# A fused attention and gated-FFN block on one core: five instruction lists written in a new order

## The chip, the core and the metric

The kernel runs on one core of a Trainium2 chip. The core's engines work side by side: TensorE (PE, matrix multiply; its weight loads are shown as PEld), VectorE (DVE), ScalarE (ACT), GpSimd (POOL) and SyncE (SP, which here only issues DMA transfers). Each takes its own list of instructions strictly in order and waits on semaphores for the others. The metric is the time of one execution on the device in microseconds, as the median of several runs.

## The reference

x has 2048 rows of 512 values, in bf16. One layer norm feeds two branches, and their results are added to x:

```python
xn = _layernorm(x)
return x + _A_ref(xn, A_wqkv, A_wo) + _B_ref(xn, B_w_gate, B_w_up, B_w_down)

# branch A: attention, 32 heads of 16; each position sees itself and
# 7 earlier ones at distances 2, 4, ... 14
qkv    = xn @ wqkv
logits = einsum("bhsd,bhswd->bhsw", q, kg) * 16 ** -0.5     # masked before the start
attn   = softmax(logits)
A      = einsum("bhsw,bhswd->bhsd", attn, vg) @ wo

# branch B: gated FFN of width 1376
B      = (gelu(xn @ w_gate) * (xn @ w_up)) @ w_down
```

## The kernel before

**Blocks.** The 2048 rows are worked in four blocks of 512 (b = 0 to 3). x comes in as eight pieces p = 0 to 7 of 256 rows, two per block; pieces 0 and 1 in two halves each. A task name carries the block or the row tile: ld_x3 is the load of piece 3, norm6 the last step of the layer norm of the sixth 128-row tile, counted from 0.

**A block's work.** The layer norm of x goes over DVE (blocks 0 and 1: bnst, bnag, sub, rstd, norm) or ACT (blocks 2 and 3), with the root on ACT or POOL (sq). Its result is transposed into xnT: in block 0 by PE (tpx, L899) and copied out of PSUM by ACT (evx, L919) and DVE (evy); in the other blocks by a DMA transpose on SP (trx p_t, L882). PE then computes

- q and k of block 0 per 128 rows (mma, mmt; L959), everything else of q, k, v in groups of four matmuls of 512 columns (mm b_which_g; which is 0 for q, 1 for k, 2 for v; L1009),
- gate and up products (fg b_j, fu b_j, j = 0 to 9; L1221; a last narrow piece fg b_10, L1260, and its up part inside er),
- the logits' sums over the products that DVE made (er b_3, L1078 and L1085),
- the down and output projections per 128 rows (acca, accb, accd, accw, L1306).

ACT moves PSUM results to SBUF (evq, evk, evv at L1020 or L986; gelu L1231; uev L1238 and L1276; fe L1339) and does the softmax's exp and ln. DVE makes the attention's products and sums (pr L1040, pa L1053, pv L1188, pw L1197, pz L1203), the softmax's other steps (mask, d1, d2, d4, d6), the gated product h (L1245) and the last additions fin. SP issues all transfers: the loads, ss (L1168) and sl (L1180), which send the probabilities to a scratch tensor in DRAM and back in spread form, ldxr (x again, for the last addition) and sto (the result).

**Memory that is shared.** PSUM has eight banks, handed out to mm, fg, fu, er (three at once) and acc groups in turn; a group can start only when the bank that it gets was emptied by ACT or DVE. x pieces have four slots in SBUF (XIN), xnT has three blocks.

**The order.** The program is not written out by loops. `G.task` collects 712 tasks with what they read and write; the dictionary ORDER gives, by hand, one list of names for each engine; `G.schedule` walks the lists with the planner's durations and latencies to find the order in which slots come free, and so which slot each item gets; `G.assign_sync` derives the semaphore waits; `emit_engine` writes each engine's instructions in the order of its list. The planner's numbers reach the chip only through the choice of slots and the waits that follow from it. The loads issue from SP in list order, and a wait of one holds all behind it:

```python
for (s, v) in t.waits:
    e.wait_ge(s, v)
ins = t.emit(e)
ins.then_inc(t.sem, 16 if eng_name == "sp" else 1)
```

A gate-weight load is also made to wait for the key weights:

```python
t_w = G.task("sp", "ld_w%s0" % nm, 0, mk(), wr=[I_w], prio=R_WG + (nm == "u"), nbytes=1280 * 1024)
t_w.deps.add(t_ld["wk"])
```

ld_wt0, ld_wt1 and ld_wt2 are the last 96 columns of the gate weights and 32 and 64 of the up weights.

Of the kernel before, what the change touches and what calls it, by code (L numbers as in the profile page):

```python
# [9 lines left out]
    LAT_X=0.08,  # L10
    LAT_S=0.03,
    TOL=dict(pe=0.6, act=-0.3, dve=0.0, pool=0.0, sp=0.0),
    DMA_ISSUE=0.48,
    DMA_FIXED=2.0,
    DMA_BPUS=330e3,
    ACT_SWITCH=1.35,
    PE_SLACK=0.0,
    PE_MODE_SWITCH=0.115,
    PE_DRAIN=0.2,
    DRAIN=0.1,  # L20
    PE_COLD_F=2.0,
    HAM_TAU=4.0,
    HAM_ENTER=0.52,
    HAM_EXIT=0.30,
)


class PeClock:

    def __init__(self, prm):  # L30
        self.tau = prm["HAM_TAU"]
        self.enter = prm["HAM_ENTER"]
        self.exit = prm["HAM_EXIT"]
        self.f = prm["PE_COLD_F"]
        self.avg = 0.0
        self.t = 0.0
        self.warm = False

    def run(self, start, dur, util):
        import math  # L40
        if start > self.t:
            self.avg *= math.exp(-(start - self.t) / self.tau)
            if self.warm and self.avg < self.exit:
                self.warm = False
            self.t = start
        left = dur
        total = 0.0
        while left > 1e-9:
            step = min(left, 0.2)
            real = step * (1.0 if self.warm else self.f)  # L50
            a = math.exp(-real / self.tau)
            self.avg = self.avg * a + util * (1.0 - a)
            if not self.warm and self.avg > self.enter:
                self.warm = True
            elif self.warm and self.avg < self.exit:
                self.warm = False
            total += real
            left -= step
        self.t = start + total
        return total  # L60

# [74 lines left out]
class Graph:  # L136
# [70 lines left out]
    def schedule(self, orders, params=None):  # L207
        prm = dict(PARAMS)
        prm.update(params or {})
        LAT_X, LAT_S = prm["LAT_X"], prm["LAT_S"]  # L210
# [12 lines left out]
        efree = dict((e, 0.0) for e in ENGS)  # L223
        act_table = None
        pe_mode = None
        pe_clock = PeClock(prm)
        dma_free = 0.0

        def rdy(t, p, od):
            if p.eng == t.eng and (p.eng == "pe" or od):  # L230
                return p.end
            return p.done + (LAT_S if p.eng == t.eng else LAT_X)

# [33 lines left out]
        for _ in range(len(self.tasks)):  # L267
# [23 lines left out]
            elif t.eng == "pe":  # L291
                sw = 0.0
                if t.mode is not None:
                    if pe_mode not in (None, t.mode):
                        sw = prm["PE_MODE_SWITCH"]
                    pe_mode = t.mode
                t.end = est + sw + pe_clock.run(est, t.dur, t.util)
                t.done = t.end + prm["PE_DRAIN"]
            else:
                t.end = est + t.dur  # L300
                t.done = t.end + prm["DRAIN"]
                if t.eng == "act" and t.table is not None:
                    act_table = t.table
# [85 lines left out]
    def report(self):  # L389
# [17 lines left out]
        "warm14 mma0_0 tpx0_1 mmt0_0 mmt0_1 mmt1_0 tpx1_0 mmt1_1 mmt0_2 tpx1_1 mmt1_2 mmt0_3 mmt1_3 "  # L407
        "mm0_2_2_0 mm0_2_1_0 fg0_0 mm0_2_0_0 fg0_1 fg0_2 fg0_3 fu0_0 fu0_1 mm0_2_3_0 fg0_4 fu0_2 fu0_3 fu0_4 "
        "fg0_5 mm1_1_0_0 mm1_0_0_0 fu0_5 fg0_6 er0_3 mm1_0_1_0 mm1_1_1_0 fg0_7 mm1_1_3_0 mm1_0_2_0 mm1_2_3_0 "
        "fg1_0 mm1_0_3_0 mm1_1_2_0 fg1_1 fu1_0 fu1_1 fu0_6 fu0_7 fg1_2 fu1_2 mm1_2_2_0 mm1_2_1_0 fg1_3 fu1_3 "  # L410
        "fg0_8 fg1_4 fu0_8 mm1_2_0_0 fg1_5 fg0_9 fu1_4 fu0_9 fu1_5 fg1_6 fg0_10 fu1_6 mm2_0_0_0 mm2_1_0_0 "
        "mm2_1_1_0 mm2_0_2_0 er1_3 fg1_7 mm2_0_3_0 mm2_0_1_0 fg1_8 mm2_1_3_0 mm2_2_0_0 fg2_0 mm2_1_2_0 accd2 "
        "fu1_7 accd1 mm2_2_2_0 fu1_8 acca0 fg1_10 mm2_2_3_0 accb0 fg2_1 fg2_2 accd3 fg2_3 fu2_0 fg1_9 fu2_1 "
        "mm2_2_1_0 fu2_2 fu2_3 er2_3 mm3_1_0_0 mm3_1_3_0 fu1_9 mm3_0_0_0 mm3_1_2_0 mm3_0_2_0 mm3_2_1_0 "
        "mm3_0_1_0 mm3_1_1_0 fg3_0 mm3_0_3_0 fg2_4 mm3_2_0_0 mm3_2_2_0 mm3_2_3_0 fu3_0 fu2_4 fg2_5 fg2_10 "
        "accd7 fu2_5 fg3_1 fu3_1 fg3_2 accd5 acca4 er3_3 fg2_6 accb4 accd6 fu2_6 fg2_7 fg2_8 fg3_10 fu2_7 "
        "fu3_2 fu2_8 fg3_3 fg3_4 fu3_3 fg3_5 fg2_9 fu2_9 fu3_4 fg3_6 fu3_5 fg3_7 fu3_6 fu3_7 fg3_8 fg3_9 "
        "fu3_8 accd11 acca8 accd10 fu3_9 accd9 accb8 acca12 accd13 accd14_0 accd14_1 accw14_0 accw14_1 "
        "accw13 accd15_0 accb12 accw15_0 accw12 accd15_1 accw15_1 accd15_2 accw15_2",
    "act":  # L420
        "c_tbl sx1 sq0 negm1 sxx1 sq1 evx0_0 evx0_1 evq0_0 sq2 evq0_1 evk0_0 evx1_0 sq3 evk0_1 bnst8 evx1_1 "
        "bnst9 evq0_2 evk0_2 evq0_3 evk0_3 ve8 sq6 vp8 sq4 bnag8 evv0_2_0 evv0_1_0 halo1 bnag9 evv0_0_0 va8 "
        "gelu0_0 bnst10 gelu0_2 uev0_0 bnst11 ve10 evv0_3_0 gelu0_1 vp10 gelu0_3 uev0_3 uev0_1 bnag10 "
        "evk1_0_0 evq1_0_0 gelu0_5 bnag11 gelu0_4 uev0_5 uev0_4 uev0_2 vb8 evq1_1_0 evk1_1_0 gelu0_6 gelu0_7 "
        "exp0 sub8 va10 evq1_2_0 vb10 ln0 sub11 d5_0 evk1_3_0 evq1_3_0 evv1_3_0 uev1_0 evk1_2_0 sub9 uev1_1 "
        "uev0_6 uev0_7 gelu1_1 gelu1_0 evv1_1_0 sub10 norm9 uev0_10b gelu1_3 evv1_2_0 gelu0_8 norm10 norm8 "
        "uev1_2 gelu1_2 norm11 gelu1_5 uev1_3 gelu1_4 bnst12 gelu0_9 uev0_9 uev1_5 uev0_8 uev0_10a bnst13 "
        "uev1_6 uev0_10c evv1_0_0 evq2_0_0 gelu0_10 evk2_1_0 ve12 evk2_0_0 vp12 evq2_2_0 bnag12 gelu1_6 "
        "uev1_4 evq2_3_0 gelu1_7 bnag13 evq2_1_0 halo2 evk2_3_0 exp1 bnst14 va12 bnst15 vb12 ve14 evk2_2_0 "
        "vp14 uev1_10b bnag14 ln1 uev1_7 d5_1 sub13 halv1 fe2 bnag15 uev1_8 va14 vb14 sub15 sub12 fe1 "  # L430
        "uev1_10c evv2_2_0 sub14 norm12 norm13 fe0 evv2_3_0 evv2_0_0 gelu2_2 gelu2_1 norm14 fe3 norm15 halo3 "
        "uev1_10a gelu2_0 gelu1_10 uev2_1 evv2_1_0 uev2_0 uev2_3 uev2_2 gelu1_8 uev2_10b uev2_10c gelu2_3 "
        "gelu1_9 evq3_0_0 evk3_0_0 evq3_2_0 evk3_3_0 evk3_2_0 evq3_1_0 exp2 halv2 evk3_1_0 uev1_9 evv3_0_0 "
        "evv3_3_0 ln2 evv3_2_0 evq3_3_0 d5_2 evv3_1_0 uev3_0 halv3 gelu2_5 uev2_10a gelu2_4 uev2_5 uev2_4 "
        "uev3_1 fe5 gelu2_10 gelu3_1 fe7 fe4 uev3_10c gelu3_2 gelu3_0 exp3 uev3_10b uev2_6 uev2_7 fe6 ln3 "
        "uev3_2 d5_3 uev2_8 gelu2_6 uev3_3 gelu2_7 gelu2_9 uev2_9 gelu2_8 gelu3_4 gelu3_5 uev3_5 gelu3_3 "
        "gelu3_6 uev3_6 uev3_4 uev3_7 gelu3_7 fe11 gelu3_10 fe10 gelu3_9 uev3_10a uev3_9 gelu3_8 uev3_8 fe8 "
        "fe9 fe13 fe12",
    "dve":
        "c_wdz bnst0 bnag0 sub0 rstd0 norm0 mean1 sub1 evy0_0 rstd1 norm1 evy0_1 bnst2 bnag2 sub2 rstd2 "  # L440
        "norm2 bnst3 bnag3 sub3 rstd3 norm3 bnst6 bnst4 bnst5 bnst7 bnag6 bnag5 bnag4 bnag7 sub4 sub5 sub6 "
        "sub7 pr0_1 rstd6 rstd4 norm7 norm5 norm6 pr0_0 norm4 pr0_3 pr0_2 pa0_0 pa0_1 pr1_0 mask d1_0 h0_1 "
        "d2_0 pr1_1 h0_2 d4a_0 d4b_0 d4c_0 pa1_0 d6_0 pr1_3 pr1_2 h0_3 rstd8 pa1_1 h0_0 h1_0 rstd10 pv0_1 "
        "pv0_0 pv0_2 pw0_1 h1_1 pv0_3 pw0_2 h0_4 d1_1 pw0_3 d2_1 pz0 h0_10 pr2_0 d4a_1 pr2_1 d4b_1 d4c_1 "
        "pr2_2 d6_1 pr2_3 pa2_0 rstd12 pa2_1 h1_3 fin2 h1_2 pv1_0 rstd14 pv1_2 pv1_3 pv1_1 h1_10 pw1_1 d1_2 "
        "pw1_2 d2_2 pw1_3 pr3_0 d4a_2 pz1 d4b_2 h1_4 d4c_2 pr3_2 pr3_3 fin1 d6_2 pr3_1 h2_0 pa3_0 pa3_1 fin0 "
        "h2_1 pa3_2 pv2_1 d1_3 h2_10 d2_3 fin3 pv2_0 h2_2 d4a_3 pv2_2 d4b_3 h3_0 d4c_3 pw2_1 d6_3 pw2_2 fin7 "
        "pv2_3 h2_3 pw2_3 h2_4 fin6 pz2 pv3_1 pv3_2 fin4 pv3_0 pv3_3 h3_2 fin11 h3_3 fin5 pw3_1 h3_1 h3_10 "
        "h3_4 fin10 pw3_2 fin8 pw3_3 fin9 pz3 fin14_0 fin14_1 fin13 fin15_0 fin15_1 fin12 fin15_2",
    "pool":  # L450
        "c_ones c_onef c_id c_vnpad c_idb c_eps c_mhalf c_e8a c_e8b c_e8c c_e8d c_ktpad c_mask0 c_mask1 "
        "c_utz sq8 sq10 sq12 sq14",
    "sp":
        "ld_x0_0 ld_x0_1 ld_wq ld_x1_0 ld_wk ld_x1_1 ld_wv ld_x2 ld_x4 ld_x3 ld_wg0 ld_wu0 ld_wt0 ld_wt1 "
# [10 lines left out]
def d_mm(n, cnt=1):  # L465
    return cnt * max(64, n) * 0.4213e-3


def d_act(n):
    return 0.10 + 0.00085 * n  # L470
# [10 lines left out]
def bass_parallel_sum__sliding_local_dilated__glu_gated_geglu__prompt_kernel(nc, A_x, A_wqkv, A_wo, B_x, B_w_gate, B_w_up, B_w_down, out, dbg=None, cfg=None):  # L481
# [42 lines left out]
    with contextlib.ExitStack() as es:  # L524
# [60 lines left out]
        G = Graph()  # L585
# [136 lines left out]
        for p in range(NP):  # L722
# [20 lines left out]
            def tp0(t, b=b, base=base):  # L743
                return -200 + 10 * t if b == 0 else base
# [676 lines left out]
```

## Time and profile before

| what | value |
|---|---|
| time, median of 3 runs | 184.19 us (184.12 to 184.24) |
| span of the profiled execution, first to last instruction | 182.8 us |
| PE busy | 178.0 us, 97% |
| DVE busy | 168.8 us, 92% |
| ACT busy | 129.3 us, 71% |
| POOL busy | 11.1 us, 6% |
| granted TensorE clock, mean | 0.999 |
| read from HBM, written to it | 14.71 MB, 3.15 MB |

The span leaves out 1.4 us around the instructions that the time has. PE's busy time counts a pipelined matmul until its modelled end, so two groups of four overlap by 0.16 us: a group lasts 1.03 us and the next starts after 0.863. Where the text gives the start of a single task, it is its first instruction's in the trace, matched to the name by its place in the engine's list.

### The profile page before, as it was taken

The numbers are of one execution on the slowest core, as the hardware profiler recorded it, in microseconds if no ns is written. First come the engines' busy times: TensorE is split into PE (matmuls) and PEld (weight loads), VectorE is DVE, ScalarE is ACT, GpSimd is POOL, SyncE is SP. The second block draws the span as 40 slices with busy tenths as digits, with TensorE's granted clock in tenths as the row PEclk, the third lists the DMA queues.
The fourth block names the chain that finished last, engine by engine and source line by source line (L and its number), as shares of the span: only waits on it lengthen the run. The fifth ranks groups of instructions, "written<-read, shape, count | busy, mean of one in ns | idle before, by whom it ended". The sixth has DMA issues, their size and how long they took to land.

```text
span 182.8 us, 2777 instructions
## 1 busy us (share of the span) xinstructions
PE 178.0 (97%) x1060; PEld 89.8 (49%) x1060; DVE 168.8 (92%) x169; ACT 129.3 (71%) x266; POOL 11.1 (6%) x23
## 2 busy tenths in 40 slices
PE   8799999999999999999999999999999999999994
PEld 2685444554444544444444555444444444444673
DVE  3769999999999999999999989999999999999932
ACT  5589977899899899869997596934396764145011
POOL 6000000104000000504000000000000000000000
PEclk9999999999999999999999999999999999999999
DMA  4999559610364000002742000136310246222333
GB/s 111 359 376 377 132 113 299 211 50 21 97 190 98 0 0 0 4 14 74 201 115 61 0 0 0 37 81 158 129 59 0 46 138 221 57 84 74 91 106 107
DMA packets 26220, 19.60 MB, mean 107 GB/s; under 512 B 13824, under 2 KB 23008, under 8 KB 26208
## 3 DMA queue, kind: packets, MB, share of 16 engines
q1 hardware_dynamic: 26208, 19.44, 36.3%
q8 instruction: 8, 0.13, 0.3%
q14 instruction: 4, 0.03, 0.1%
HBM read 14.71 MB, written 3.15 MB: 98 GB/s over the span
## 4 chain that ended last, share of the span: by engine, by line
PE 89%; DMA 8%; SPq 1%; issue 0%; DVE 0%; DVEq 0%
PE PS L1221 38%; PE PS L1306 28%; PE PS L1009 18%; DMA Wg<-in_B_w_gate_dram 5%; DMA Wqkv<-in_A_wqkv_dram 3%; PE PS L1260 2%; PE PS L1085 2%; PE PS L1078 1%; SPq L731 1%; SPq L687 0%; DVE OB L1350 0%; DVEq L376 0%
## 5 line engine op out<-in xcount | busy, mean ns | idle before, releaser
L1306 PE MATMUL PS<-Wd,HT 128*128 128x512 bf16 (+2 forms) x209 | 40.8, 345 | 0.0
L1221 PE MATMUL PS<-xnT,Wg 128*128 128x512 bf16 x160 | 39.6, 379 | 0.3 <-DMA Wg<-in_B_w_gate_dram 0.3
L1221 PE MATMUL PS<-xnT,Wu 128*128 128x512 bf16 x160 | 38.8, 379 | 0.0
L1009 PE MATMUL PS<-xnT,Wqkv 128*128 128x512 bf16 x160 | 37.8, 379 | 0.0
L1040 DVE TENSOR_TENSOR UNI<-QT,KT 128x4096 f16<-128x4096 bf16 x16 | 36.4, 2287 | 0.1
L1188 DVE TENSOR_TENSOR UNI<-VN,PT 128x4096 f16<-128x4096 bf16 x16 | 36.0, 2286 | 0.0
L1306 PEld LDWEIGHTS PS<-Wd,HT 128*128 128x128 bf16 x209 | 19.7, 98 | 19.0
L1238 ACT ACTIVATE UU<-PS 128x512 bf16<-128x512 f32 x40 | 22.8, 604 | 7.9 <-PE PS L1221 6.2
L1197 DVE TENSOR_TENSOR UNI<-UNI 128x4096 f16<-128x4096 f16 x12 | 27.4, 2286 | 0.0
L1009 PEld LDWEIGHTS PS<-xnT,Wqkv 128*128 128x128 bf16 x160 | 17.9, 114 | 16.9 <-ACT UU L1238 0.4
L1231 ACT ACTIVATE GG<-PS 128x512 bf16<-128x512 f32 x40 | 23.4, 600 | 2.5 <-DVE HT L1245 1.7
L1221 PEld LDWEIGHTS PS<-xnT,Wg 128*128 128x128 bf16 x160 | 15.4, 98 | 19.6 <-DMA Wg<-in_B_w_gate_dram 0.7
L1221 PEld LDWEIGHTS PS<-xnT,Wu 128*128 128x128 bf16 x160 | 15.7, 98 | 18.8
L1339 ACT ACTIVATE OB<-PS 128x512 bf16<-128x512 f32 x14 | 8.2, 594 | 21.8 <-PE PS L1306 21.8
L1053 DVE TENSOR_TENSOR UNI<-UNI 128x4096 f16<-128x4096 f16 x9 | 20.4, 2282 | 0.0
L1306 PE MATMUL PS<-Wo,OT 128*128 128x512 bf16 (+2 forms) x76 | 16.5, 345 | 0.0
L1245 DVE TENSOR_TENSOR HT<-GG,UU 128x1024 bf16<-128x1024 bf16 x20 | 13.6, 686 | 0.0
L832 POOL TENSOR_TENSOR sq<-ve,mhalf 128x2 bf16<-128x2 f32 x4 | 8.2, 2058 | 73.3 <-ACT ve L828 73.3
L1020 ACT ACTIVATE VN<-PS 128x512 bf16<-128x512 f32 x16 | 9.3, 594 | 2.5 <-PE PS L1009 2.5
L1306 PEld LDWEIGHTS PS<-Wo,OT 128*128 128x128 bf16 x76 | 7.2, 98 | 6.5
L1020 ACT ACTIVATE QT<-PS 128x512 bf16<-128x512 f32 x12 | 7.2, 597 | 3.2 <-PE PS L1009 3.2
L959 PE MATMUL PS<-xnT,Wqkv 128*128 128x128 bf16 x128 | 8.2, 219 | 1.2 <-DMA Wqkv<-in_A_wqkv_dram 1.0
(85 smaller groups left out, 153.9 us busy)
## 6 DMA issues: line engine op xcount, KB each, us to landing
PT<-pt_scratch SPq DMA_DIRECT2D x16, 256.0 KB, 4.0
XR<-in_A_x_dram SPq DMA_DIRECT2D x16, 128.0 KB, 2.4
out_dram<-OB SPq DMA_DIRECT2D x14, 128.0 KB, 2.0
Wqkv<-in_A_wqkv_dram SPq DMA_DIRECT2D x3, 512.0 KB, 5.6
XIN<-in_A_x_dram SPq DMA_DIRECT2D x6, 256.0 KB, 6.0
Wg<-in_B_w_gate_dram SPq DMA_DIRECT2D x1, 1280.0 KB, 8.8
Wu<-in_B_w_up_dram SPq DMA_DIRECT2D x1, 1280.0 KB, 11.6
Wd<-in_B_w_down_dram SPq DMA_DIRECT2D x1, 1280.0 KB, 7.7
```

The source lines that it names most:

```text
L832: "pool", "sq%d" % t, 7.0, lambda e, t=t, n=n: e.tensor_tensor(out=sq[:, t:t + n], in0=ve[:, t:t + n], in1=mhalf[:, 0:n], op=ALU.pow),
L1009: ins = e.matmul(PS[:, 512 * it.slot:512 * it.slot + 512], lhsT=wcols(which, kt, g), rhs=xnT[:, itx.slot, kt, :], start=(kt == 0), stop=(k ...
L1020: return e.activation(out=o, in_=PS[:, 512 * it.slot:512 * it.slot + 512], func=ACTF.Identity, scale=(QSC, 1.0, 1.0)[which])
L1040: return lambda e: e.tensor_tensor(out=UNI[:, it.slot, :, :], in0=bass.AP(QT, (itq.slot * 4 + g) * 512, [[NQT * 4 * 512, 128], [0, 8], [1, ...
L1053: return lambda e: e.tensor_tensor(out=UNI[:, i0.slot, :, :], in0=UNI[:, i0.slot, :, :], in1=UNI[:, i1.slot, :, :], op=ALU.add)
L1188: return lambda e: e.tensor_tensor(out=bass.AP(UNI, ito.slot * 4096, [[NUNI * 4096, 128], [2048, 2], [512, 4], [1, 512]]), in0=bass.AP(VN, ...
L1197: return lambda e: e.tensor_tensor(out=UNI[:, i0.slot, :, :], in0=UNI[:, i0.slot, :, :], in1=UNI[:, i1.slot, :, :], op=ALU.add)
L1221: ins = e.matmul(PS[0:M, 512 * it.slot:512 * it.slot + 512], lhsT=Wx[:, kt, j * 128:j * 128 + M], rhs=xnT[:, itx.slot, kt, :], start=(kt = ...
L1231: return lambda e: e.activation(out=GG[:, ito.slot, q, :], in_=PS[:, 512 * it.slot:512 * it.slot + 512], func=ACTF.Gelu_apprx_tanh)
L1238: return lambda e: e.activation(out=UU[:, ito.slot, q, :], in_=PS[:, 512 * it.slot:512 * it.slot + 512], func=ACTF.Identity)
L1245: return lambda e: e.tensor_tensor(out=HT[:, ito.slot, j - 1:j + 1, :], in0=GG[:, ig.slot, :, :], in1=UU[:, iu.slot, :, :], op=ALU.mult)
L1306: ins = e.matmul(PS[:, 512 * it.slot:512 * it.slot + CW], lhsT=(OT[:, ito.slot, q, ti * 128:(ti + 1) * 128] if kind == "o" else HT[:, ith. ...
```

## The change

All five lists of ORDER hold the same names as before, and the bodies of all tasks are the same. Four lists are in a new order (POOL's is only wrapped differently), and the planner's numbers are changed: its durations of single tasks, its latencies, starting times and DMA rates, and the clock model of PE is taken out. One consequence is that items can get other slots.

In SP's list ld_x3 comes ahead of ld_x1_1 and ld_x2, ld_wv behind ld_x2, and ld_x4 behind ld_wv, directly ahead of ld_wg0 as ld_x3 was. ld_x5, which stood directly behind ld_wt1, now stands behind the first transpose trx3_0. The lists, cut to their heads and to what the text speaks of:

```diff
     "pe":
-        "warm14 mma0_0 tpx0_1 mmt0_0 mmt0_1 mmt1_0 tpx1_0 mmt1_1 mmt0_2 tpx1_1 mmt1_2 mmt0_3 mmt1_3 "
-        "mm0_2_2_0 mm0_2_1_0 fg0_0 mm0_2_0_0 fg0_1 fg0_2 fg0_3 fu0_0 fu0_1 mm0_2_3_0 fg0_4 fu0_2 fu0_3 fu0_4 "
-        "fg0_5 mm1_1_0_0 mm1_0_0_0 fu0_5 fg0_6 er0_3 mm1_0_1_0 mm1_1_1_0 fg0_7 mm1_1_3_0 mm1_0_2_0 mm1_2_3_0 "
...
-        "accd7 fu2_5 fg3_1 fu3_1 fg3_2 accd5 acca4 er3_3 fg2_6 accb4 accd6 fu2_6 fg2_7 fg2_8 fg3_10 fu2_7 "
-        "fu3_2 fu2_8 fg3_3 fg3_4 fu3_3 fg3_5 fg2_9 fu2_9 fu3_4 fg3_6 fu3_5 fg3_7 fu3_6 fu3_7 fg3_8 fg3_9 "
-        "fu3_8 accd11 acca8 accd10 fu3_9 accd9 accb8 acca12 accd13 accd14_0 accd14_1 accw14_0 accw14_1 "
-        "accw13 accd15_0 accb12 accw15_0 accw12 accd15_1 accw15_1 accd15_2 accw15_2",
+        "warm14 mma0_0 tpx0_1 mmt0_0 mmt0_1 mmt1_0 tpx1_0 mmt1_1 mmt0_2 tpx1_1 mmt1_2 mmt0_3 mm0_2_0_0 mmt1_3 "
+        "mm0_2_2_0 mm0_2_1_0 fg0_0 fg0_1 fg0_2 fg0_3 fu0_0 fu0_1 fu0_2 fg0_4 fu0_3 mm1_0_0_0 mm1_1_0_0 "
+        "mm0_2_3_0 fg0_5 fu0_4 fg0_6 mm1_1_1_0 er0_3 mm1_0_1_0 fg1_0 fg0_7 mm1_1_2_0 fu0_5 mm1_1_3_0 "
...
+        "mm3_1_1_0 fg2_7 fu3_1 accd7 fg3_2 fg3_3 fu3_2 mm3_2_2_0 acca4 er3_3 fg3_4 accb4 accd5 fu2_7 "
+        "mm3_2_1_0 fg3_5 fu3_3 fg2_8 fu2_8 fu3_4 accd6 fg3_6 fg3_10 fu3_5 fg2_9 fg3_7 fu3_6 fu2_9 fu3_7 fg3_8 "
+        "fu3_8 fg3_9 fu3_9 acca8 accb8 accd9 accd10 accd11 accd14_0 accd13 accd14_1 acca12 accw14_0 accw13 "
+        "accw14_1 accb12 accw12 accd15_0 accw15_0 accd15_1 accw15_1 accd15_2 accw15_2",
     "act":
-        "c_tbl sx1 sq0 negm1 sxx1 sq1 evx0_0 evx0_1 evq0_0 sq2 evq0_1 evk0_0 evx1_0 sq3 evk0_1 bnst8 evx1_1 "
-        "bnst9 evq0_2 evk0_2 evq0_3 evk0_3 ve8 sq6 vp8 sq4 bnag8 evv0_2_0 evv0_1_0 halo1 bnag9 evv0_0_0 va8 "
-        "gelu0_0 bnst10 gelu0_2 uev0_0 bnst11 ve10 evv0_3_0 gelu0_1 vp10 gelu0_3 uev0_3 uev0_1 bnag10 "
...
-        "gelu3_6 uev3_6 uev3_4 uev3_7 gelu3_7 fe11 gelu3_10 fe10 gelu3_9 uev3_10a uev3_9 gelu3_8 uev3_8 fe8 "
+        "c_tbl sx1 sq0 negm1 sxx1 sq1 evx0_0 evx0_1 evq0_0 sq2 evx1_0 sq3 evk0_0 evq0_1 evk0_1 evx1_1 evq0_2 "
+        "bnst8 evk0_2 sq4 evq0_3 sq6 bnst9 evk0_3 ve8 vp8 bnag8 halo1 bnag9 evv0_2_0 gelu0_0 gelu0_3 gelu0_2 "
+        "evv0_0_0 bnst10 uev0_0 uev0_1 bnst11 va8 uev0_2 gelu0_1 gelu0_4 ve10 evq1_0_0 vp10 uev0_3 bnag10 vb8 "
...
+        "d5_3 gelu3_5 gelu3_4 fe6 uev2_8 gelu2_8 uev3_4 uev3_5 gelu2_9 uev3_10b evv3_1_0 gelu3_6 uev2_9 "
+        "gelu3_7 uev3_7 uev3_6 gelu3_10 uev3_9 uev3_10c uev3_10a uev3_8 gelu3_9 fe8 gelu3_8 fe9 fe10 fe11 "
     "dve":
-        "norm2 bnst3 bnag3 sub3 rstd3 norm3 bnst6 bnst4 bnst5 bnst7 bnag6 bnag5 bnag4 bnag7 sub4 sub5 sub6 "
-        "sub7 pr0_1 rstd6 rstd4 norm7 norm5 norm6 pr0_0 norm4 pr0_3 pr0_2 pa0_0 pa0_1 pr1_0 mask d1_0 h0_1 "
...
-        "pv2_3 h2_3 pw2_3 h2_4 fin6 pz2 pv3_1 pv3_2 fin4 pv3_0 pv3_3 h3_2 fin11 h3_3 fin5 pw3_1 h3_1 h3_10 "
-        "h3_4 fin10 pw3_2 fin8 pw3_3 fin9 pz3 fin14_0 fin14_1 fin13 fin15_0 fin15_1 fin12 fin15_2",
+        "bnst3 bnag3 sub3 rstd3 norm3 bnst6 bnst4 bnst5 bnag6 bnag4 bnag5 bnst7 sub5 sub4 bnag7 sub6 sub7 "
+        "rstd4 rstd6 norm5 norm7 norm6 norm4 pr0_2 pr0_3 pr0_0 pr0_1 pa0_1 h0_0 pa0_0 pr1_0 mask rstd8 d1_0 "
...
+        "d6_3 pw2_1 h3_1 fin6 pw2_2 h3_2 pw2_3 h2_4 h3_0 h3_3 pz2 pv3_1 pv3_0 fin8 pv3_3 h3_4 h3_10 pv3_2 "
+        "pw3_1 fin10 pw3_2 fin11 pw3_3 fin9 pz3 fin14_0 fin14_1 fin13 fin15_0 fin12 fin15_1 fin15_2",
     "sp":
-        "ld_x0_0 ld_x0_1 ld_wq ld_x1_0 ld_wk ld_x1_1 ld_wv ld_x2 ld_x4 ld_x3 ld_wg0 ld_wu0 ld_wt0 ld_wt1 "
-        "ld_x5 trx3_1 trx2_1 trx3_0 trx2_0 ld_wt2 ld_x6 ld_wd0 ldxr2 ld_x7 ld_wd1 ldxr1 ld_wo ss0_0 ss0_1 "
-        "ss0_3 ss0_2 sl0_1 sl0_0 sl0_2 trx4_1 sl0_3 trx5_0 trx4_0 trx5_1 ss1_0 ss1_3 ss1_2 ss1_1 sl1_0 sl1_2 "
-        "sl1_3 trx6_1 trx6_0 sl1_1 trx7_0 trx7_1 ldxr0 sto2 sto1 ldxr6 ss2_0 ss2_1 ss2_3 ss2_2 sl2_1 sl2_0 "
...
+        "ld_x0_0 ld_x0_1 ld_wq ld_x1_0 ld_wk ld_x3 ld_x1_1 ld_x2 ld_wv ld_x4 ld_wg0 ld_wu0 ld_wt0 ld_wt1 "
+        "trx3_0 ld_x5 trx3_1 ld_wt2 trx2_0 trx2_1 ld_x6 ld_wd0 ss0_3 ss0_2 ss0_0 ss0_1 ld_wd1 sl0_1 sl0_2 "
+        "sl0_0 sl0_3 ld_wo ld_x7 trx4_1 trx4_0 trx5_0 trx5_1 ldxr0 ss1_3 ss1_2 ss1_0 ss1_1 sl1_1 ldxr2 sl1_0 "
+        "sl1_2 sl1_3 trx7_0 ldxr3 trx6_1 trx7_1 ldxr1 trx6_0 ldxr7 ss2_1 sto0 ss2_2 ss2_0 ss2_3 sl2_0 sto1 "
...
-SCHED = dict(DMA_BPUS=290e3, DMA_FIXED=1.7)
...
-        G.schedule(ORDER, SCHED)
+        G.schedule(ORDER)
```

## The prediction

> **What bounds the kernel now.** I read the page's busy line first, then the chain of waits, then the timelines of PE, ACT, DVE and SP over the first 30 us.
>
> From the page, each engine's busy time:
>
> ```profile
> PE 178.0 (97%) x1060; PEld 89.8 (49%) x1060; DVE 168.8 (92%) x169; ACT 129.3 (71%) x266; POOL 11.1 (6%) x23
> ```
>
> PE has 4.8 us without work in 182.8, DVE 14. From the chain that ended last (start us, length us, what):
>
> ```profile
> 2.75 5.60 DMA Wqkv<-in_A_wqkv_dram
> 8.35 0.02 issue
> 8.37 8.76 DMA Wg<-in_B_w_gate_dram
> 17.13 0.05 issue
> 17.17 1.04 PE PS L1221 x4
> 18.21 0.86 PE PS L1009 x4
> ...
> 24.25 4.32 PE PS L1221 x20
> 28.57 1.73 PE PS L1009 x8
> ...
> 163.53 16.75 PE PS L1306 x122
> ```
>
> The key weights land at 8.35 and release the gate weights, which land at 17.13. From 17.17 to 180.28 the chain is PE alone, with no wait between pieces. A reordering can't shorten this stretch: the same matmuls, at 0.863 us for a group of four, take the same 163 us. What can be won is PE work moved ahead of 17.17. What can be lost is any wait inside the stretch. The PE timeline just before it:
>
> ```profile
> 12.04 3.16 PE L959 MATMUL PS<-xnT,Wqkv 128*128 128x128 bf16 x48
> 15.03 1.89 PE L1009 MATMUL PS<-xnT,Wqkv 128*128 128x512 bf16 x8
> 17.17 1.04 PE L1221 MATMUL PS<-xnT,Wg 128*128 128x512 bf16 x4 [0.25 <-DMA Wg<-in_B_w_gate_dram]
> ```
>
> The two L1009 groups could have been followed by a third at 15.03 + 2 x 0.863 = 16.75; PE stood until 17.17, so 0.42 us. Smaller waits hide in the merged rows: the L959 batch mmt0_2 starts at 10.89, behind the first ACT row here, and mmt0_3 at 13.22, behind the last. ACT's timeline:
>
> ```profile
> 10.25 0.59 ACT L919 ACTIVATE xnT<-PS 128x512 bf16<-128x512 bf16 x1
> ...
> 11.96 0.63 ACT L769 ACTIVATE XS<-XIN 128x512 bf16<-128x512 bf16 x1 [0.45 <-DMA XIN<-in_A_x_dram]
> ...
> 12.59 0.58 ACT L919 ACTIVATE xnT<-PS 128x512 bf16<-128x512 bf16 x1
> ```
>
> evx1_0 (10.25) and evx1_1 (12.59) move transposed x out of PSUM. The second stands behind bnst8, which waited for x4. From DVE's timeline:
>
> ```profile
> 12.71 2.47 DVE L750 BATCH_NORM_STATS2 st<-XIN 128x6 f32<-128x512 bf16 x4 [1.10 <-DMA XIN<-in_A_x_dram]
> ```
>
> DVE waits 1.10 us for x3, which is in the queue behind x4. And from SP's timeline, the loads ld_wt1, ld_x5, the four block-1 transposes and ld_wt2:
>
> ```profile
> 9.99 2.62 SPq L703 DMA_DIRECT2D Wt<-in_B_w_up_dram  x1
> 12.66 4.04 SPq L737 DMA_DIRECT2D XIN<-in_A_x_dram  x1
> 19.26 5.23 SPq L882 DMA_TRANSPOSE xnT<-XIN  x4
> 24.53 0.58 SPq L703 DMA_DIRECT2D Wt<-in_B_w_up_dram  x1
> ```
>
> An issue of these kinds takes 0.43 to 0.6 us when nothing holds it. ld_wt1 ends at 12.61 as x3 lands (12.68), ld_x5 at 16.70 as Wg lands (17.13): SP is let in only when an older load is nearly down.
>
> **The change, part by part.** Durations are those of the profiled execution; its span of 182.8 stands 1.4 below the median of 184.19, and I add each difference in the span to the median.
>
> *Planner numbers, durations, byte counts.* No instruction comes or goes; they cost 0, and act only through the slots and waits that the planner derives.
>
> *Head, loads.* The weight and x bytes queued ahead of Wg are the same, and Wg still waits for wk (8.35), so I keep 17.13 for Wg and 20.41 for Wu. The rows' landings give 0.75 us per 256 KB (x2 11.18, x4 11.93, x3 12.68) and 0.35 for the 128 KB behind wk. In the new order: x3 9.10, x1_1 9.45 (was 8.70), x2 10.2, wv 11.9 (was 10.43), x4 12.7. x4 now takes the slot that waits for tpx0_1, as x3 did.
>
> *Head, ACT and DVE.* bnst3 starts at 9.5 instead of 9.25. sq3 no longer stands behind evk0_0, so norm3 ends near 11.35 (was 11.61), and bnst6 starts at 11.25 instead of 12.71. All four block-1 norms now stand ahead of the first pr0: from 11.25, 2.4 (four bnst) + 0.33 (bnag) + 1.05 (sub) + 0.2 + 1.05 (norm) give 16.3, and norm6, third of them, about 16.2 (was 19.75). evx1_0 starts at 10.0 and ends 10.57; evx1_1 follows three evictions from 10.65 and ends 12.66.
>
> *Head, PE.* mmt0_2 at 10.67 (-0.22); mmt0_3 at 12.71 (a batch costs 0.89, a transpose 0.23); then mm0_2_0_0, new ahead of Wg and with wv long landed, mmt1_3, and two L1009 groups: 12.71 + 0.92 + 0.86 + 0.89 + 0.86 + 0.86 = 17.10. Wg is there at 17.17, so fg0_0 starts as before, but mm0_2_0_0 (was at 18.05) is done. **Gain 0.86**; bounds 0.5, if PE gets there 0.35 late, and 0.9, which is the three waits together (0.22 + 0.29 + 0.42). fu0_0, four groups on, is at 20.62, 0.2 behind Wu.
>
> *Block 1 brought forward.* In the new PE list nine groups lie between 17.17 and mm1_0_0_0 (fg0_0 to fg0_3, fu0_0 to fu0_2, fg0_4, fu0_3): 17.17 + 9 x 0.863 = 24.94. Before, the first block-1 group was at 28.41, 2.7 us behind the last transpose's landing (25.73). Now all four transposes must be down by 24.9, and PE, in order, does nothing else meanwhile. On SP, trx3_0 takes the place directly behind ld_wt1 and stands ready at 16.2; then ld_x5, trx3_1, ld_wt2, trx2_0, trx2_1: each transpose 1.26, x5 0.45, wt2 0.6. *If nothing is held after 16.70*: trx3_0 ends 17.9, x5 18.4, trx3_1 19.65, wt2 20.25, trx2_0 21.5, trx2_1 22.8; a transpose lands 1.24 after its issue ends (24.49 to 25.73), so 24.05, and PE waits 0. *If x5 is held until Wu is down*, as the two held rows suggest (each went in with three weight pieces or so still unlanded; here Wu, two Wt pieces and a transpose are ahead): x5 ends about 20.0, trx3_1 21.25, wt2 21.85, trx2_0 23.15, trx2_1 24.45, landed 25.7; PE waits 0.8. I take the second, since two rows show it, and keep 0 and 1.2 (landing at 26.1, held until the Wt pieces land as well) as ends.
>
> [...]
>
> *ld_x5 later.* ACT's bnst10 stands behind gelu0_0, gelu0_3, gelu0_2 and evv0_0_0, at 22.4; x5 lands at 22.1 to 23.0 (issue end + 2.0 to 2.9, the latter as for x6, 25.67 to 28.53). ACT then runs back to back to about 58 in the new list. Counting banks at these spacings, PE still finds one of the 8 in time if x5 is down by 23.1, later by whatever PE has already waited. Cost 0; beyond, 1 us per us.
>
> *The later lists.* ACT keeps its table loads (sqrt, then gelu and exp in turn per block), er and acc groups are as many, DVE has 1.2 us in hand from the head. ldxr, ss and sl issues follow their data: ss0 starts with d6_0 at about 42 (was 43.46), so sl0_1 lands before 50.7, when pv0_1 wants it; trx5_1 lands near 60.5, mm2_1_0_0 is at 61.6; ldxr1 is put ahead of trx6_0, which still lands near 98, 4 us early. These cost 0, hidden by PE's own run. Two relays become tight: pa3_2 to er3_3 (0.66 before, about 0.25 now) and pz2 to acca8 (4.5 before). The latter: from fu3_7's start to acca8's PE has 5 x 0.863 = 4.32 us; ACT and DVE need until then 0.2 (fu2_9's end) + 0.48 x 3 (uev2_9, gelu3_7, uev3_7) + 0.60 (uev3_6) + 0.64 (h3_3) + 1.22 (pz2) + 0.1 (handoffs) = 4.2. I take 0 for both, with 0.4 as the upper end. The tail behind accw14_0 is the same chain of fin and store: 0.
>
> *Sum.* -0.86 + 0.8 + 0 = -0.06: 184.19 - 0.06 = 184.1. With the ends: -0.9 gives 183.3; -0.5 + 1.2 + 0.4 gives 185.3.
>
> **The rivals.**
>
> *B, the transposes land in time.* For it: trx3_1 in the old trace, issued at 19.26 with Wu unlanded, took 1.30 against 1.19 to 1.27 elsewhere, so hardly held. Against: by then Wu was nearly through. PE keeps the gain and, earlier everywhere, meets tighter banks and relays: -0.86 + 0.2 = 183.5.
>
> *C, the relay at acca8.* h3_3 is late by more than 0.15, since ACT or DVE has one more 0.5 us eviction or part of a 2.2 us product ahead, and PE waits for pz2 just ahead of accd9. It decides from 0.15 on, 1 us per us: at 0.7 late, with A's stall, 184.1 + 0.55 = 184.7. For it: DVE at 92% has no room to catch up, and the slack went from 4.5 us to 0.15. Against: my spacings are medians and the list may have room that I don't see.
>
> *D, x5 or the transposes later still*, landing past 26.5: 185.1.
>
> *That the change does not do what is said*: in SP's list x4 stays ahead of ld_wg0, and what moves is x5, from directly behind ld_wt1 to behind trx3_0. Both places are behind the gate weights. If that move counted for nothing, the head alone would remain, which is B.
>
> **How the numbers follow.** A, head gained and lost again at mm1_0_0_0: 0.42, within 183.7 to 184.6, time **184.1**. B 0.25, C 0.25, D 0.08. For eight in ten the range takes A, most of B and C up to 0.9 late: 183.4 to 185.0. About 0.2%, 0.37 us, is what a measurement here tells from no change. Faster, below 183.82: 0.21 of B and 0.08 of A, 0.29. Slower, above 184.56: 0.22 of C, 0.08 of D, 0.07 of A, 0.37. Within: 0.34.
>
> **What would show it.** PE: fg0_0 near 17.2 behind three L1009 groups instead of two, with no wait at mmt0_3 (else the head is wrong). A PE wait on a DMA of xnT near 25 of 0.3 to 1.2 (A); none (B). SP: the issue of x5 longer than 1.5 us, ending near 20 (A), or 0.45 long (B). ACT's wait for x5 below 0.7. Waits of PE L1306 or L1085 on DVE after 120 mean C. Wg landing away from 17.13 by more than 0.4 would upset the sum at its root.

## The result, and the profile after

The changed kernel is slower: 185.03 us median (184.87 to 185.25, 5 runs) against 184.24 for the kernel before beside it, ratio 1.0042, 95% interval 1.0029 to 1.0054. On a second occasion it was 184.78 (12 runs) against 184.04 (17 runs), 1.0036 (1.0021 to 1.0050). The forecast was 184.1, no change. One execution of all those below ran at a lower granted clock (0.991, 188.62 us) and is left out of the second experiment's figures. In the two profiles shown here PE was through earlier than before: its last group starts at 179.42 (before 179.88). That lead belongs to the profile before, whose gate weights landed late; in three later profiles of the old order the group starts at 178.86 to 179.41. PE's end does not show where the time went.

From the page after, each engine's busy time:

```profile
PE 177.2 (97%) x1043; PEld 89.8 (49%) x1060; DVE 169.0 (92%) x169; ACT 128.3 (70%) x266; POOL 18.4 (10%) x23
```

The work is the same; 17 matmul records are missing, so PE's figure is low by them, and PE's tasks below are placed by the weight loads, of which none is missing. POOL's 7 us more are its four sq tasks, one of them above all (last section). From the chain that ended last (start us, length us, what):

```profile
17.74 2.37 SPq L839
...
22.02 2.80 DMA xnT<-XIN
24.82 0.05 issue
24.87 2.78 PE PS L966 x12
...
126.07 2.21 DVE UNI L1010
128.28 0.04 issue
128.32 0.62 PE PS L1035 x16
```

Before, the chain ran over PE alone from 17.17 on. Now it enters PE at 24.87 from a transpose (mm1_0_0_0 waits for trx2_1) and at 128.32 from DVE (er3_3 waits for pa3_2). PE's timeline at the start of both stretches:

```profile
13.52 0.81 PE L966 MATMUL PS<-xnT,Wqkv 128*128 128x512 bf16 x3
14.16 1.06 PE L916 MATMUL PS<-xnT,Wqkv 128*128 128x128 bf16 x16
15.06 1.89 PE L966 MATMUL PS<-xnT,Wqkv 128*128 128x512 bf16 x8
16.78 3.62 PE L1178 MATMUL PS<-xnT,Wg 128*128 128x512 bf16 x16
...
128.32 0.62 PE L1035 MATMUL PS<-xnT,Wt 128*32 128x256 bf16 x16 [0.26 <-DVE UNI L1010]
```

Three groups (L966) now stand ahead of fg0_0, as forecast, and fg0_0 starts at 16.78, 0.24 behind the gate weights. SP's timeline, from the first transpose on (trx3_0, ld_x5, trx3_1, ld_wt2, trx2_0 and trx2_1 together with the gap between them):

```profile
15.76 1.30 SPq L839 DMA_TRANSPOSE xnT<-XIN  x1
17.11 0.57 SPq L694 DMA_DIRECT2D XIN<-in_A_x_dram  x1
17.74 2.37 SPq L839 DMA_TRANSPOSE xnT<-XIN  x1
20.15 0.58 SPq L660 DMA_DIRECT2D Wt<-in_B_w_up_dram  x1
20.78 2.90 SPq L839 DMA_TRANSPOSE xnT<-XIN  x2
```

SP's held issue ends at 20.11, 0.29 behind the landing of the up weights (19.82), but it is trx3_1, not ld_x5. Then the end. The DMA view of 180.2 to 183.2 us, first of the kernel before (queue, kind, packets, MB, share; then the issues: KB each and us from issue to landing):

```profile
q1 hardware_dynamic: 432, 0.20, 22.7%
...
out_dram<-OB SPq DMA_DIRECT2D x1, 32.0 KB, 1.6
```

and of the changed kernel:

```profile
q1 hardware_dynamic: 384, 0.15, 18.3%
q14 instruction: 1, 0.01, 0.6%
...
out_dram<-OB SPq DMA_DIRECT2D x1, 32.0 KB, 2.4
```

The last store, sto15_2, takes 2.4 us instead of 1.6, and there is a packet of another kind: 8 KB of *instructions*. By the packet records it starts at 181.31 and takes 0.31; behind it the last eight of the store's 128 data packets go out from 181.61 to 181.77, when all others had ended by 181.34. The store lands 2.08 us after its issue ended, 1.13 before. In the kernel before a packet of this kind comes at 184.54, 1.8 us behind the last instruction. A hint of where it comes from is in the lists: the new order makes DVE wait for more semaphores in instructions of their own, 193 instructions in DVE's trace instead of 188. ACT's has seven more too, 293 instead of 286.

### The profile page after: what moved, and what is told of

Read it like the earlier page. It is cut to its first block, busy times and chain, and to the rows that moved or that the text cites. A ratio compares the mean times of both kernels' runs of the same rounds, so it can differ in the third digit from the quotient of the medians.

```text
span 183.1 us, 2768 instructions
## 1 busy us (share of the span) xinstructions
PE 177.2 (97%) x1043; PEld 89.8 (49%) x1060; DVE 169.0 (92%) x169; ACT 128.3 (70%) x266; POOL 18.4 (10%) x23
## 4 chain that ended last, share of the span: by engine, by line
PE 34%; DVE 21%; ACT 20%; issue 11%; POOLq 4%; SPq 3%; DMA 3%; POOL 0%; DVEq 0%
PE PS L1263 18%; PE PS L1178 10%; DVE UNI L1010 5%; DVE UNI L1145 5%; POOLq L481 4%; DVE UNI L997 4%; ACT GG L1188 3%; DVE UNI L1154 3%; PE PS L966 3%; ACT UU L1195 3%; SPq L839 3%; PE PS L916 2%; DMA xnT<-XIN 2%; ACT XIN L810 1%; ACT XS L726 1%
## 5 line engine op out<-in xcount | busy, mean ns | idle before, releaser
L1178 PE MATMUL PS<-xnT,Wg 128*128 128x512 bf16 x158 | 38.9, 379 | 0.3 <-issue 0.2
L966 PE MATMUL PS<-xnT,Wqkv 128*128 128x512 bf16 x155 | 37.9, 379 | 0.5 <-issue 0.2
L966 PEld LDWEIGHTS PS<-xnT,Wqkv 128*128 128x128 bf16 x160 | 17.8, 114 | 17.2 <-DMA xnT<-XIN 0.6
L1195 ACT ACTIVATE UU<-PS 128x512 bf16<-128x512 f32 x40 | 23.3, 608 | 2.7 <-PE PS L1178 2.7
L789 POOL TENSOR_TENSOR sq<-ve,mhalf 128x2 bf16<-128x2 f32 x4 | 15.6, 3898 | 66.3 <-ACT ve L785 66.3
L977 ACT ACTIVATE KT<-PS 128x512 bf16<-128x512 f32 x12 | 7.1, 598 | 2.0 <-PE PS L966 2.0
```

Of the source, the lines that this page charges most:

```text
L789: "pool", "sq%d" % t, 3.0, lambda e, t=t, n=n: e.tensor_tensor(out=sq[:, t:t + n], in0=ve[:, t:t + n], in1=mhalf[:, 0:n], op=ALU.pow),
L966: ins = e.matmul(PS[:, 512 * it.slot:512 * it.slot + 512], lhsT=wcols(which, kt, g), rhs=xnT[:, itx.slot, kt, :], start=(kt == 0), stop=(k ...
L977: return e.activation(out=o, in_=PS[:, 512 * it.slot:512 * it.slot + 512], func=ACTF.Identity, scale=(QSC, 1.0, 1.0)[which])
L1178: ins = e.matmul(PS[0:M, 512 * it.slot:512 * it.slot + 512], lhsT=Wx[:, kt, j * 128:j * 128 + M], rhs=xnT[:, itx.slot, kt, :], start=(kt = ...
L1195: return lambda e: e.activation(out=UU[:, ito.slot, q, :], in_=PS[:, 512 * it.slot:512 * it.slot + 512], func=ACTF.Identity)
```

## The experiments

Theory F: the end of DVE's stream now calls for the next 8 KB of instructions, and they stand in front of the last store. Rivals: a stray late landing (L), the new order of the last stores (S), ACT's stream (A).

**The changed kernel once more.**

> The changed kernel once more, for a second profile. In the first, PE was through 0.46 us earlier than in the kernel before (last group started at 179.42 against 179.88), but the last store landed 2.09 us after its issue ended (1.13 before), with an 8 KB instruction packet of 0.31 us at 181.31, just ahead of the store's last packets. Theory F (the end is held by that instruction packet): the packet is there again near 181 and the last store lands again 1.8 to 2.4 us after its issue; time 185.0, about 0.8 above the kernel before. Rival L (a stray late landing of one execution): the last store lands 1.1 to 1.3 us after its issue and the span is near 182.2. Apart from that: the key weights landed at 7.80 against 8.35 with the same loads ahead of them; if that belongs to the execution and not to the order, they land elsewhere in 7.7 to 8.5 here, and the first gate group starts 9.0 us behind them.

Measured: 184.78. The packet is there again (180.78), the store lands 1.86 us after its issue: L is out. The key weights landed at 7.70, the gate weights at 16.20. Here mm1_0_0_0 did not wait at all. Executions of one kernel differ in such things: the spans of the 12 runs lie at 182.4 to 182.6 (five) and at 183.0 to 183.6 (seven). The two profiles, one of each group, differ by 0.31 at mm1_0_0_0 and by 0.2 in the store's landing.

**More waits, without effect but to lengthen a list.** Two of these satisfied waits share one instruction: 40 make 20 (the trace has 20 more):

```diff
+            if eng_name == "dve" and t.name == "pv3_1":
+                for _ in range(40):
+                    e.wait_ge(*t.waits[-1])
             ins = t.emit(e)
```

> The changed kernel with 20 more wait instructions in DVE's list, all satisfied, ahead of pv3_1 where DVE stands idle for 0.97 us. Theory F, with DVE's stream as the one that is fetched (193 instructions in the trace against 188 before, so that its end passes a boundary of the stream): the 8 KB packet moves to about 160 to 170 us, the last store lands 1.1 to 1.3 us after its issue, and the time falls by 0.8 to 1.3 to 183.8 to 184.3. Rival S (the new order of the last stores makes it late) and rival A (ACT's stream): 185.0 as for the changed kernel, the packet still near 181.

Measured: 185.70, ratio 1.0094 (1.0074 to 1.0114). The time is a miss, by the experiment's own doing: the waits stand behind pv3_1's own wait, at 0.098 us each, so DVE lost 2.0 us and PE waited 1.9 us for pz3 at accw14_0. But the packet moved to 165.50, and the last store lands 1.12 us after its issue. From the DMA views of 164 to 168 and of 180.2 to 184:

```profile
q14 instruction: 1, 0.01, 0.5%
```

```profile
out_dram<-OB SPq DMA_DIRECT2D x2, 32.0 KB, 1.5
```

So the packet belongs to DVE's stream, and the late landing to the packet; S, which has the same order of stores here, is out.

The same with ACT, ahead of fe13:

> The changed kernel with 20 more satisfied wait instructions in ACT's list, ahead of fe13, where ACT stands idle for 7.5 us. Theory F with DVE's stream and rival S: nothing changes, 185.0, the packet near 181. Rival A (the packet belongs to ACT's stream, 293 instructions against 286): the packet moves to before 175 and the time falls to 183.8 to 184.3.

Measured: 185.21 (1.0075, 1.0059 to 1.0090), the packet at 180.70, the store 1.85 us after its issue. A is out. The 0.4 more are again the waits, which made fe13 start 1.15 us later and with it the last stores.

The kernel before with ten such waits (five instructions) ahead of fin14_0, so that DVE's list is as long as the changed one:

> The kernel before with 5 more wait instructions in DVE's list, all satisfied, ahead of fin14_0, where DVE stands idle for 1.16 us: its list is then as long as the changed kernel's. Theory F with DVE's stream: an 8 KB instruction packet appears between 180.5 and 182.5, the last store lands 1.8 to 2.4 us after its issue, and the time rises by 0.8 to 1.3 to 185.0 to 185.5, with no instruction of the kernel moved. Rivals S, A and L: 184.2 as before.

Measured: 184.80 against 184.04, ratio 1.0041 (1.0028 to 1.0053). With the old order, every instruction at its place, the whole loss of the change is there (0.76; 0.8 to 1.3 was expected). The DMA view of 180.2 to 183.2:

```profile
q14 instruction: 1, 0.01, 0.8%
...
out_dram<-OB SPq DMA_DIRECT2D x1, 32.0 KB, 2.4
```

These are the two lines of the changed kernel's view: an instruction packet, and 2.4 us to the landing. The packet starts at 181.29; sto15_2's issue ends 1.25 us behind the start of PE's last group, as before (1.26), so fin14_0's half microsecond cost nothing, and the landing alone is later, by 0.85.

**The packet moved out of the way**, with the waits now ahead of those in which DVE stands idle anyway:

```diff
+        last = None
...
+            if eng_name == "dve" and t.name in PAD:
+                for _ in range(2 * PAD[t.name]):
+                    e.wait_ge(*last)
+            last = t.waits[-1] if t.waits else last
             for (s, v) in t.waits:
...
+PAD = {'rstd14': 4, 'pv3_1': 9}
```

> The changed kernel with 13 more satisfied wait instructions in DVE's list, now placed ahead of the waits that DVE stands in anyway: 4 ahead of rstd14 (0.39 us at 0.098 each, in 0.58 idle) and 9 ahead of pv3_1 (0.88 in 0.97 idle). The 20 waits of the first try stood behind pv3_1's own wait and cost 1.96 us. Theory F (DVE's 188th to 191st instruction calls for the next 8 KB of its stream; at the end of the list this holds the last store): the packet is at 172 to 175, the last store lands 1.1 to 1.2 us after its issue, the time falls by 0.7 to 1.0 below that of the changed kernel, to 183.8 to 184.1, the same as the kernel before. Rival: 184.8 as the changed kernel.

Measured: 183.90 against 184.00, ratio 1.0001 (0.9986 to 1.0015). The packet is at 174.91, the store lands after 1.11. From the DMA views of 173 to 177 and of 180.2 to 183.2:

```profile
q14 instruction: 1, 0.01, 0.8%
```

```profile
out_dram<-OB SPq DMA_DIRECT2D x1, 32.0 KB, 1.4
```

A hit: with the packet away the changed kernel takes as long as the kernel before. The gain over the changed kernel is 0.88 by the medians and 0.65 by the means, since that kernel's runs stand in two groups.

And in the kernel before, with `PAD = {'d4a_2': 5, 'fin14_0': 10}`:

> The kernel before with 15 more satisfied wait instructions in DVE's list, 5 ahead of d4a_2 and 10 ahead of fin14_0, both in idle time. In the kernel before the packet comes at 184.54, after the last instruction, and 1.9 us of its time lie outside the span against 1.73 for the kernels with the packet inside. Theory F with a price outside the span too: the packet moves to 174 to 176, the last store still lands 1.1 us after its issue, and the time falls by 0.2 to 183.8. Rival (the packet after the end costs nothing): no change within 0.1.

Measured: 183.63, ratio 0.9984 (0.9971 to 0.9996). Time less span is 1.70 to 1.79 here (median 1.74), 1.79 to 2.08 (median 1.91) in the kernel before beside it: the packet 1.8 us behind the last instruction had a price of about 0.2 too. The rest of the 0.37 is within the span and open. So of the changed kernel's loss the packet accounts for about 0.9 in the span, less the 0.2 that it cost before outside. The fairer comparison of the two orders, both with the packet moved, is 183.90 to 183.63: the new order is 0.27 dearer, though the two intervals overlap, and with the packet in front of the last store both orders take 184.8.

A smaller dose, two more instructions ahead of fin14_0 in the kernel before:

> The kernel before with 2 more satisfied wait instructions in DVE's list, ahead of fin14_0 in idle time: 190 instructions in the trace where 188 left the packet behind the end and 193 brought it in front of the last store. Theory F: either the packet is inside the span and the last store lands 1.8 us or more after its issue, and the time is 184.6 to 184.9, or it isn't, and the time is 184.0; nothing between. By the kernel with 20 waits, where the packet came 1.4 us behind the 189th instruction, the first is the likelier. Rival (each wait instruction has a price of its own): 184.3, in proportion to the 5 that cost 0.76.

Measured: 183.74 against 183.98 (0.9985, 0.9972 to 0.9997). Neither number of theory F nor the rival's: the packet came at 183.04, 1.1 us behind the last instruction instead of 1.8, and 0.2 of the time outside the span is gone. Five instructions cost 0.76, two gain 0.24: it is the place of the packet that counts, not the number of waits. Which instruction calls for it is open; with 190 in the list it came after the end, with 193 before.

**Where the head's gain went.** In the kernel with the packet moved, what PE waited for between 14 and 173.5 us (us in total, times, longest):

```profile
PE PS L1042 <- DVE UNI L1017: 0.4, 1, 0.4
```

One wait, er3_3 for pa3_2. Across five profiles of the changed order acca4 and this wait last 3.23 to 3.47 us, 2.90 in the old. There is a second place, here by the profile of the changed kernel: pz3 ends at 173.23 and accw14_0 starts at 173.29, 2.02 behind acca12, which takes 1.94 where nothing holds PE (2.09 with the packet moved). DVE had lost 0.97 us on its way there:

```profile
152.13 1.22 DVE L1160 TENSOR_TENSOR OT<-UNI 128x2048 bf16<-128x2048 f16 x1
154.32 4.49 DVE L1145 TENSOR_TENSOR UNI<-VN,PT 128x4096 f16<-128x4096 bf16 x2 [0.97 <-DMA PT<-pt_scratch]
```

pv3_1 wants sl3_1, which SP issues behind sl3_0, sl3_3 and a store. So sl3_1 first:

```diff
-... ss3_0 ss3_1 sl3_0 sl3_3 sto4 sl3_1
+... ss3_0 ss3_1 sl3_1 sl3_0 sl3_3 sto4
+PAD = {'rstd14': 4, 'fin14_0': 11}
```

> The changed kernel with sl3_1 ahead of sl3_0, sl3_3 and sto4 in SP's list, and the packet moved by 4 waits ahead of rstd14 and 11 ahead of fin14_0. In the changed kernel DVE stands 0.97 us at pv3_1 for the landing of sl3_1 (154.30), pz3 ends at 172.95 to 173.23, and PE's accw14_0 starts 0.06 behind it, 0.2 later than PE could. Theory R (DVE's end releases PE there): pz3 ends 0.8 to 1.0 earlier, PE goes from acca12 to accw14_0 without a wait, 0.2 less than the kernel with only the packet moved, about 183.7. Rival (PE is not held there): the same time as that kernel.

Measured: 183.84 (0.9993, 0.9984 to 1.0002), no clear gain over 183.90. pz3 ends at 172.36, accw14_0 follows acca12 after 1.94; that part of R holds, though only 0.1 to 0.15 was to be had there, not 0.2. But PE's end is no earlier, since in this execution er3_3 waited longer:

```profile
PE PS L1042 <- DVE UNI L1017: 0.7, 1, 0.7
```

DVE was 0.4 later at pa3_2, with 0.26 more waiting at pv0_3 and 0.17 more at mask. Then also er3_3 one group later:

```diff
-... mm3_2_2_0 acca4 er3_3 fg3_4 accb4
+... mm3_2_2_0 acca4 fg3_4 er3_3 accb4
```

> As the kernel with sl3_1 first, and er3_3 one group later in PE's list (behind fg3_4 instead of ahead of it). In three profiles of the changed kernel er3_3 starts 0.06 behind the end of pa3_2 (128.27, 127.98), and acca4 with the wait behind it takes 3.23 to 3.39 us against 2.90 in the kernel before. Theory E (er3_3 gives back 0.33 to 0.49 of the head's gain): no wait there, PE's end earlier by 0.3 to 0.5, time 183.2 to 183.5, below both kernels. Rival (DVE, which waits for er3_3 at d1_3, sets the end): pz3 ends later by what er3_3 is later, and the time stays at 183.7.

Measured: 183.74 (0.9987, 0.9972 to 1.0001). A miss: the wait at er3_3 is gone, the time is not. PE's and ACT's timelines show the next one:

```profile
137.72 1.04 PE L1185 MATMUL PS<-xnT,Wg 128*128 128x512 bf16 x4 [0.31 <-ACT EX L1097]
```

```profile
135.35 1.28 ACT L1096 ACT_TABLE_LOAD   x1 [0.70 <-DVE PS L1086]
136.64 1.02 ACT L1097 ACTIVATE EX<-PS 128x1024 f16<-128x1024 f32 x1
```

fg2_8 now waits, 0.48 by the starts (the view counts from the modelled end of the group ahead), for the PSUM banks of the logits, which exp3 empties, which waited for DVE's step d2_3. By these profiles the stretch from pa3_2 to exp3 goes at DVE's pace, and PE, being ahead, meets it at one place or the next.

**The head alone.** If this is so, the head should pay in the old order, where the profile before has 0.70 us between pa3_2 and er3_3 and 0.43 between pz3 and accw14_0:

```diff
 pe   -... mmt0_3 mmt1_3 mm0_2_2_0 mm0_2_1_0 fg0_0 mm0_2_0_0 fg0_1
      +... mmt0_3 mm0_2_0_0 mmt1_3 mm0_2_2_0 mm0_2_1_0 fg0_0 fg0_1
 act  the changed list as far as bnag8, then the old one
 dve  the changed list as far as norm4, then the old one
 sp   -... ld_wk ld_x1_1 ld_wv ld_x2 ld_x4 ld_x3 ld_wg0
      +... ld_wk ld_x3 ld_x1_1 ld_x2 ld_wv ld_x4 ld_wg0
+PAD = {'d4a_2': 5, 'fin14_0': 10}
```

> The kernel before with the head alone of the change: the loads in the new order as far as ld_wt1, PE's mm0_2_0_0 ahead of the gate weights, ACT's list in the new order as far as bnag8, DVE's as far as norm4 (all four block-1 norms ahead of the first product); everything behind it as before, block 1 at its old place, and the packet moved to about 175 as in the kernel before with the packet moved (183.63). In profiles with the gate weights at 16.0 to 16.7 the changed kernel's fg0_0 started at 16.61 to 16.76, the old order's 0.04 to 0.15 behind the landing, so the head is worth 0.863 less 16.7, plus the landing and 0.04: 0.2 to 0.85, 0.45 at 16.3. Theory H (the head's gain is real and was given back at er3_3 and accw14_0, where the old order has 0.70 and 0.43 to spare): 183.63 - 0.45 = 183.2, range 183.0 to 183.4, no wait at er3_3. Rival (DVE paces the end whatever PE does): 183.6.

Measured: 183.14 against 183.98, ratio 0.9955 (0.9942 to 0.9968), below both kernels. Theory H: 0.49 less than the old order with the packet moved, and the two intervals do not touch. PE's timelines, the old head and the new:

```profile
14.44 1.89 PE L1016 MATMUL PS<-xnT,Wqkv 128*128 128x512 bf16 x8
16.16 1.03 PE L1228 MATMUL PS<-xnT,Wg 128*128 128x512 bf16 x4
17.02 1.03 PE L1016 MATMUL PS<-xnT,Wqkv 128*128 128x512 bf16 x4
```

```profile
14.90 1.89 PE L1016 MATMUL PS<-xnT,Wqkv 128*128 128x512 bf16 x8
16.63 3.62 PE L1228 MATMUL PS<-xnT,Wg 128*128 128x512 bf16 x16
```

The new head starts fg0_0 0.47 later with one group of 0.863 less to do: 0.39 by these two profiles, and PE's end is 0.40 earlier (178.46 against 178.86). Nothing of it is given back: er3_3 has its 0.70 still (pa3_2 ends at 126.59, er3_3 starts at 127.29).

## Why the prediction was wrong

**The step that failed** is the tail, "The tail behind accw14_0 is the same chain of fin and store: 0", and with it the sentence "No instruction comes or goes". That holds for the instructions that compute. But the new order brings five wait instructions into DVE's list, and these are part of a stream that is itself fetched by DMA: with 20 more of them in the changed kernel the 8 KB instruction packet moved from 181.31 to 165.50, with 13 more to 174.91. The runs put 0.76 in the place of 0 (old order with five more waits), and 0.88 comes back when the packet is moved in the changed kernel (184.78 to 183.90). The trace before shows eight instruction packets of 16 KB and four of 8 KB within the span, and the one at 184.54 behind it; the prediction names none. That the extra waits come from the order and not from the planner's numbers can be counted in two further programs, which were not run: the new order with the old numbers has as many in DVE's list as the changed kernel, the old order with the new numbers as many as before. What the new slots alone do to the time no run tells.

**The sum of the other steps** came out near, in part by luck. With the packet away the changed kernel takes 183.90, against 184.00 for the kernel before and 183.63 for that kernel with its packet away too, so 0.10 less or 0.27 more where 0.06 less was forecast. Its terms moved, and their errors went both ways:

- *Head, 0.86.* The size was off, the mechanism right: 0.49 by the run of the head alone. The profile of the kernel before has the latest gate weights of all twelve profiles (17.13; the others 16.01 to 16.66, with the same bytes ahead). There PE's 0.42 us of waiting was large. With 16.3 the old order starts fg0_0 at about 16.3 and the new one at 16.7, when PE is ready, 0.4 behind the weights. That is the case of the lower bound, 0.5. The same profile is why the 1.4 us between span and median were not the kernel's: its span is 182.1 in the middle of 17 runs, and 1.9 us lie outside.
- *Block 1 forward, 0.8.* Measured 0.31, 0.14 and five times 0 in seven profiles. SP was held, as the two old rows suggested: the held issue ended 0.2 to 0.3 behind the landing of the up weights in all seven (20.11 against 19.82, 19.81 against 19.50). But ld_x5 went through in 0.57 and trx3_1 was held, so trx3_1 no longer stood behind the held issue, and trx2_1 landed at 24.2 to 24.8 (25.03 in one execution), not 25.7.
- *ld_x5 later, 0.* Right: it landed at 21.3 to 21.6, ahead of bnst10.
- *The later lists, 0.* Wrong at er3_3, where I found 0.25 in hand: 0.33 to 0.57 in five profiles, about the upper end of 0.4. I had reckoned DVE 1.2 us ahead from the head. Its first product starts at 15.97 (old order 16.13 with like loads), and between there and pz3 it stands idle 2.2 us against 1.0. The wait at accw14_0, 0 to 0.15, I did not name. acca8, rival C's place, had no wait.

Of the rivals, C had the right kind of loss (a DVE relay late in the run) at the wrong place; D's 185.1 was the right time for a wrong reason. No case had the packet.

## What to carry to other kernels

Reordering can change the number of wait instructions (here five more on DVE, seven more on ACT), so compare the length of each engine's list, and look for instruction packets near the last store; a few satisfied waits in an idle place moved such a packet here (13 of them from 181.31 to 174.91). Whether one delays a transfer that PE waits for was not tried here. A gain read from one profile as a difference of two landings holds for that execution: here the landings differed by 1.1 us between profiles, and the head was worth 0.49, not 0.86. And work won early is worth only what the tightest relay behind it has to spare: the same head gave 0.49 with 0.70 in hand at er3_3. In the changed order, with nothing in hand there, the waits at er3_3 took about as much again; no run takes the head out of that order, so that it gave nothing there is argued, not shown.

## What the hardware showed that I had not expected

- An 8 KB instruction packet of 0.31 to 0.73 us made the last store land 0.7 to 0.95 later: 1.84 to 2.08 us behind its issue in the four profiles that have the packet there, 1.11 to 1.14 in the eight others. In the changed kernel 0.43 of that is the late data; the rest is between the store's last packet and its landing, 0.87 against 0.35, and what takes it is open.
- A wait instruction with two satisfied waits took 0.098 us on DVE and 0.077 on ACT in the two runs with 20 of them in a row.
- POOL's sq on 128x2 elements took from 0.71 to 7.46 us. In the changed kernel sq14 starts at 78.29 and ends at 85.74, 0.55 behind the end of an unbroken row of DVE's work, and DVE's rstd14 then waits 0.58 for it; the task takes 7.45 to 7.46 in all seven profiles of the new order, 2.07 to 2.08 in the five of the old. No run was made on its cause.
